# Top-32 attention and a gated feed-forward layer: shifts of exp on ScalarE, late reads, one reciprocal a duo

## The chip, the cores and the metric

The kernel runs on one core of a Trainium2 chip. The core has five engines with queues of their own, each of which works its instructions in order: TensorE (matmul, PE in the profile), VectorE (DVE), ScalarE (ACT), GpSimd (POOL) and SyncE (SP), which issues the transfers. The metric is the device time of one execution in microseconds, the median of several runs.

## What is computed

```python
# q, k, v: (8, 8, 576, 64)
scores = (1 / sqrt(64)) * q @ k.transpose(0, 1, 3, 2)
kth    = 32nd largest score of each row
scores = where(scores >= kth, scores, -1e9)
attn   = exp(scores - max(scores))
attn   = attn / (sum(attn) + 1e-9)
x      = (attn @ v), heads side by side      # (4608, 512)
h      = x @ w_in                            # (4608, 2048)
g      = h * clip(h + 3, 0, 6) / 6
out    = g @ w_out                           # (4608, 512)
```

The two weight matrices arrive as 64-bit floats; the kernel makes 32-bit floats of them itself, out of the two 32-bit words of each.

## The kernel before, in words

**Tiling.** There are 8 batches of 8 heads. Two heads make a pair, so a batch has 4 pairs. The 576 rows of a head are four tiles of 128 rows and a rest of 64. A *duo* is two pairs (four heads) at one tile of rows. `Duo` has an index `u` (0 or 1) for the pair and `t` (0 or 1) for the head in the pair. A duo of the rest has half as much to do. A batch has 8 full duos and 2 of the rest; there are 80 duos.

**One duo.** `scores` has TensorE write scores into the one large PSUM tile (`big`, one buffer), and ScalarE copies them to `sc` in SBUF (L233, L236). `top` finds the 32 largest of each row on VectorE with four rounds of MAX8 (L250) and three of MATCH_REPLACE8 (L254). `shift` forms (32nd largest - largest) x scale, on GpSimd (L263, L266). `exp` on ScalarE flattens what lies below the 32nd value (L273), takes the exponential with its sum into `den` (L278) and adds a small constant (L283). `inverse` is VectorE's reciprocal of `den` (L287). `weights` on GpSimd multiplies by it (L297) and splits the 32-bit words into 16-bit halves (L306). `flip` transposes these by a transfer (L312), and `join` puts the halves together again as `eT` (L318), on ScalarE for u = 0 and on GpSimd for u = 1. `values` multiplies them with v on TensorE (L338, `pv`), and `place` has ScalarE copy the result into `xT` (L348), or `xr` for rests.

**Feed-forward.** 128 finished rows make a block. `feed_forward` is a generator that is worked in 16 pieces: 8 pieces compute `h` (L365), 512 columns in every two pieces, then 8 sum `acc` over w_out (L385). After each 512 columns of h, ScalarE reads h twice (L373, L375); `gate` on GpSimd follows two pieces later (L379, L380). After the last piece, ScalarE scales `acc` into `o` (L395), and SyncE writes it out.

**Order of the work.** It is written out by hand, and no scheduler changes it. Each duo has 8 slots, one for each round of `top`; the loop at L564 goes through them. The tables `usual`, `behind`, `early`, `soon` (L532 to L545) say at which slot, counted from the duo's first, each step of the duo is issued; a number over 7 is a slot of a later duo. A slot issues the round of `top`, the steps that are due (`parts`, those named shift first), a step of the weights' conversion as long as there is one, at slot 1 the scores of the next duo, and then pieces of feed-forward: about one a slot, somewhat more if over 24 pieces are left (L597). So values of a duo stand at its slot 22 (`usual`), or at slot 25 and thus behind the scores issued at slot 25 (`behind`, from the second batch on until four duos from the end).

**Conversion.** `convert` loads 512 columns (L102), takes the magnitude and the low word on ScalarE into `a` and `y` (L108, L111), clamps on GpSimd (L109), and combines on VectorE (L117, L118) and GpSimd (L123). There are 16 pieces of w_in, then 16 of w_out, one step each slot during the first four duos.

Of the kernel before, what the change touches and what calls it, by code (L numbers as in the profile page):

```python
# [16 lines left out]
TOP_K = 32  # L17
# [12 lines left out]
def kernel(  # L30
# [65 lines left out]
    def convert(dst, src):  # L96
# [10 lines left out]
        y = gpool.tile([P, WC], F32, tag="g", name="y")  # L107
# [7 lines left out]

        au, yu = a[:].bitcast(U32), y[:].bitcast(U32)
        nc.vector.tensor_scalar(au, au, 3, None, ALU.logical_shift_left)  # L117
        nc.vector.scalar_tensor_tensor(  # L118
            out=yu, in0=hi, scalar=0x80000000, in1=yu,
# [4 lines left out]
            dst.bitcast(I32), a[:].bitcast(I32), y[:].bitcast(I32), ALU.add  # L124
# [14 lines left out]
    class Pair:  # L139
# [6 lines left out]
        def load(self):  # L146
            h0 = 2 * self.hp
            t = self.landed = kqpool.tile([P, 2 * J + 1, 2, D], F32, tag="kq", name="landed")
            for i, src in enumerate((k, q)):
                for hh in range(2):  # L150
                    nc.sync.dma_start(
                        t[:, i * J : (i + 1) * J, hh, :],
                        src[self.b, h0 + hh, 0:JP, :].rearrange("(p j) d -> p j d", j=J),
                    )
                nc.sync.dma_start(
# [29 lines left out]
    class Duo:  # L185
# [73 lines left out]
        def shift(self, u):  # L259

            nt, m = self.nt, self.m[u]
            d = self.less[u] = mpool.tile([P, 2], F32, tag="shift", name="shift")
            nc.gpsimd.tensor_tensor(  # L263
                d[:, 0:nt], m[:, 0:nt, TOP_K - 1], m[:, 0:nt, 0], ALU.subtract
            )
            nc.gpsimd.tensor_scalar_mul(d[:, 0:nt], d[:, 0:nt], scale)  # L266

        def exp(self, u):
# [7 lines left out]
            for t in range(nt):  # L276
                row = self.row(u, t)
                nc.scalar.activation(  # L278
                    row, row, AF.Exp, bias=self.less[u][:, t : t + 1], scale=-scale / FLAT,
                    accum_out=self.den[:, u, t : t + 1],  # L280
                )
            d = self.den[:, u, 0:nt]
            nc.scalar.activation(d, d, AF.Copy, bias=EPS)  # L283

        def inverse(self, u):
            d = self.den[:, u, 0 : self.nt]
            nc.vector.reciprocal(d, d)  # L287
# [64 lines left out]
    def feed_forward(xT, rows):  # L352
# [6 lines left out]
        for f0 in range(0, NFC, nf):  # L359
# [12 lines left out]
            g = gpool.tile([P, 512], F32, tag="g", name="g")  # L372
            nc.scalar.activation(g[:], h[:], AF.Relu, bias=three[:], scale=1.0)  # L373
            hs = hpool.tile([P, 512], F32, tag="h", name="hs")
            nc.scalar.copy(hs[:], h[:])  # L375
            gs.append(g)

            def gate(g=g, hs=hs):
                nc.gpsimd.tensor_scalar(g[:], g[:], 6.0, 0.0, ALU.min, ALU.max)  # L379
                nc.gpsimd.tensor_tensor(g[:], g[:], hs[:], ALU.mult)  # L380

            yield gate
        acc = ps_w.tile([P, DM], F32, tag="w", name="acc")
        for f in range(NFC):
# [7 lines left out]
            if f % 2 == 1:  # L392
                if f == NFC - 1:
                    o = opool.tile([P, DM], F32, tag="o", name="o")
                    nc.scalar.mul(o[:], acc[:], 1.0 / 6.0)  # L395
                    for p0, p1, dst in rows:
                        nc.sync.dma_start(dst, o[p0:p1, :])
                yield None

# [5 lines left out]
    for b in range(B):  # L405
        halves = [pairs[b][0:2], pairs[b][2:4]]
        for qt in range(J):
# [3 lines left out]
            if qt == (0 if b == B - 1 else J - 1) and not 2 < b < B - 1:  # L411
# [11 lines left out]
    gates = []  # L423

    def piece(count=1):
        nonlocal left
        for _ in range(count):
            while todo:
                try:
                    gates.append(next(todo[0]))  # L430
                    left -= 1
                    break
                except StopIteration:
                    todo.pop(0)
            else:
                gates.append(None)
            if len(gates) > 2:
                gate = gates.pop(0)
                if gate:
                    gate()  # L440
# [45 lines left out]
    def land(count=1):  # L486

        for _ in range(min(count, len(chunks))):
            c = convert(*chunks.pop(0))
# [20 lines left out]
    def pair_at(m, first):  # L510
# [5 lines left out]
    first[0].load()  # L516
# [16 lines left out]
        shift0=3, exp0=4, inverse0=9, weights0=10, flip0=12, join0=15,  # L533
        shift1=7, exp1=8, inverse1=13, weights1=14, flip1=16, join1=19, values=22, place=23,
# [101 lines left out]
```

## Time and profile before

| | |
|---|---|
| median of 3 runs | 1581.66 us (1581.61 to 1581.7) |
| span of the profiled execution | 1578.5 us |
| busy: TensorE, VectorE | 1456.9 us (92%), 1466.8 us (93%) |
| busy: GpSimd, ScalarE | 1144.5 us (73%), 1096.3 us (69%) |
| top-32: L250 and L254, all forms | 1519 us of instruction time, which overlaps |
| feed-forward on TensorE, L385 and L365 | 516.9 and 544.4 us |
| GpSimd's wait for `den` (L297) | 222.7 us |
| ScalarE's waits for h (L373) and for sums (L395) | 140.6 and 106.6 us |

How to read it: a busy share is a mean over the whole span; the slices, forty of 39.5 us each, show where it lies (a 9 is 90% or more). In lists of waits the engine and line that waited come first, then for what; the numbers are the total in us, the number of waits and the longest. In lists in order of time the columns are the start and the duration in us, the engine, the line, the operation and its operands, and in brackets the idle time before it and what ended that. TensorE's ends are modelled, so it may show as full with small gaps. A matmul of 32-bit floats shows as two records for each instruction, for instance 8 `acc` records for 4 instructions.

### The profile page before, as it was taken

The numbers are of one execution on the slowest core, as the hardware profiler recorded it, in microseconds if no ns is written. First come the engines' busy times: TensorE is split into PE (matmuls) and PEld (weight loads), VectorE is DVE, ScalarE is ACT, GpSimd is POOL, SyncE is SP. The second block draws the span as 40 slices with busy tenths as digits, with TensorE's granted clock in tenths as the row PEclk, the third lists the DMA queues.
The fourth block names the chain that finished last, engine by engine and source line by source line (L and its number), as shares of the span: only waits on it lengthen the run. The fifth ranks groups of instructions, "written<-read, shape, count | busy, mean of one in ns | idle before, by whom it ended". The sixth has DMA issues, their size and how long they took to land.

```text
span 1578.5 us, 28787 instructions
## 1 busy us (share of the span) xinstructions
PE 1456.9 (92%) x10272; PEld 1039.0 (66%) x10272; DVE 1466.8 (93%) x3105; ACT 1096.3 (69%) x1865; POOL 1144.5 (73%) x1264
## 2 busy tenths in 40 slices
PE   5256799979999999998999999999999999999899
PEld 3153566567767777666777777776777767677675
DVE  6999999999999999999999999999999999999700
ACT  6675777777777777777776786777766787777621
POOL 4868687777867777867687777867687777767841
PEclk9568999989999999999999999999999999999999
DMA  8652543444344543545254543446244443533410
GB/s 236 159 181 45 113 83 81 94 91 97 76 90 89 101 83 76 101 85 119 55 106 76 97 89 82 93 93 116 57 96 87 98 88 74 103 65 68 83 22 14
DMA packets 450319, 144.49 MB, mean 92 GB/s; under 512 B 433280, under 2 KB 441472, under 8 KB 450176
## 3 DMA queue, kind: packets, MB, share of 16 engines
q1 hardware_dynamic: 450176, 142.65, 43.5%
q8 instruction: 81, 1.33, 0.3%
q14 instruction: 62, 0.51, 0.1%
HBM read 45.09 MB, written 9.44 MB: 35 GB/s over the span
## 4 chain that ended last, share of the span: by engine, by line
DVE 51%; PE 35%; POOL 5%; issue 3%; ACT 3%; DMA 1%; SPq 1%; POOLq 0%; ACTq 0%; DVEq 0%
DVE m L250 26%; DVE wk L254 22%; PE h L365 14%; PE acc L385 13%; PE pv L338 4%; PE big L232 3%; POOL e L306 1%; DVE y L118 1%; POOL sc L297 1%; DMA t<-e 1%; POOL eT L318 1%; DVE a L117 1%; PE big L177 1%; ACT sc L278 1%; ACT eT L318 1%
## 5 line engine op out<-in xcount | busy, mean ns | idle before, releaser
L250 DVE MAX8 m<-wk 128x8 f32<-128x576 f32 x864 | 613.1, 746 | 2.2
L385 PE MATMUL acc<-w_out,g 128*128 128x512 f32 x1152 | 516.9, 600 | 14.1 <-POOL g L380 14.1
L365 PE MATMUL h<-xT,w_in 128*128 128x128 f32 x4096 | 485.5, 279 | 17.3 <-ACT xT L348 17.3
L365 PEld LDWEIGHTS h<-xT,w_in 128*128 128x128 f32 x4096 | 475.0, 195 | 39.5 <-issue 18.2
L254 DVE MATCH_REPLACE8 wk<-m,wk 128x576 f32<-128x576 f32 x576 | 423.7, 742 | 0.0
L385 PEld LDWEIGHTS acc<-w_out,g 128*128 128x128 f32 x1152 | 213.6, 191 | 260.4 <-issue 238.6
L297 POOL TENSOR_SCALAR sc<-sc,den 128x576 f32<-128x576 f32 x288 | 213.8, 753 | 229.9 <-DVE den L287 222.7
L306 POOL COPY e<-sc 128x2304 uint16<-128x2304 uint16 (+1 forms) x192 | 320.3, 1678 | 10.2
L278 ACT ACTIVATE sc<-sc,shift 128x576 f32<-128x576 f32 x288 | 220.4, 769 | 40.5 <-POOL shift L266 37.7
L318 ACT COPY eT<-t 128x2304 uint16<-128x2304 uint16 (+1 forms) x82 | 215.9, 2632 | 37.9 <-DMA t<-e 35.3
L273 ACT ACTIVATE sc<-sc,m 128x576 f32<-128x576 f32 x288 | 210.1, 777 | 46.2 <-DVE m L250 46.0
L338 PE MATMUL pv<-eT,vm 128*64 128x128 f32 (+1 forms) x2560 | 164.0, 273 | 57.9 <-ACT eT L318 45.8
L254 DVE MATCH_REPLACE8 wk<-m,sc 128x576 f32<-128x576 f32 x288 | 211.8, 742 | 0.0
L318 POOL COPY eT<-t 128x2304 uint16<-128x2304 uint16 (+1 forms) x78 | 203.8, 2613 | 6.9 <-DMA t<-e 6.5
L338 PEld LDWEIGHTS pv<-eT,vm 128*64 128x64 f32 x2560 | 135.2, 141 | 109.3 <-ACT eT L318 49.7
L250 DVE MAX8 m<-sc 128x8 f32<-128x576 f32 x288 | 203.3, 742 | 2.4 <-ACT sc L236 2.4
L373 ACT ACTIVATE g<-h,three 128x512 f32<-128x512 f32 x144 | 98.5, 684 | 150.0 <-PE h L365 140.6
L380 POOL TENSOR_TENSOR g<-g,hs 128x512 f32<-128x512 f32 x144 | 185.0, 1285 | 12.1 <-POOL g L379 0.2
L233 ACT COPY sc<-big 128x2048 f32<-128x2048 f32 (+1 forms) x65 | 119.3, 1836 | 26.1 <-PE big L232 26.0
L232 PE MATMUL big<-kq 64*128 64x512 f32 x512 | 136.4, 653 | 0.0
L379 POOL TENSOR_SCALAR g<-g 128x512 f32<-128x512 f32 x144 | 89.2, 620 | 62.6 <-ACT g L373 52.4
L395 ACT ACTIVATE o<-acc 128x512 f32<-128x512 f32 x36 | 21.4, 595 | 106.6 <-PE acc L385 106.6
(47 smaller groups left out, 1113.1 us busy)
## 6 DMA issues: line engine op xcount, KB each, us to landing
landed<-in_k_dram SPq DMA_DIRECT2D x64, 128.0 KB, 3.0
landed<-in_q_dram SPq DMA_DIRECT2D x64, 128.0 KB, 3.0
st<-in_moe_w_in_dram SPq DMA_DIRECT2D x16, 512.0 KB, 5.1
vm<-in_v_dram SPq DMA_DIRECT2D x64, 128.0 KB, 2.3
st<-in_moe_w_out_dram SPq DMA_DIRECT2D x16, 512.0 KB, 6.6
out_dram<-o SPq DMA_DIRECT2D x32, 256.0 KB, 2.4
t<-e SPq DMA_TRANSPOSE x160, 4.6
landed<-in_k_dram SPq DMA_DIRECT2D x32, 32.0 KB, 2.8
```

The lines of the kernel that those rows point to most:

```text
L232: nc.tensor.matmul(banks[:, 2 * i + hh, :], pr.qT[d, qs], pr.kT[d, :])
L250: nc.vector.max(self.m[u][:, t, 8 * r : 8 * r + 8], self.cur[t])
L254: nc.vector.match_replace(wk, self.m[u][:, t, 8 * r : 8 * r + 8], self.cur[t], LOWEST)
L273: nc.scalar.activation(row, row, AF.Prelu, bias=m[:, t, TOP_K - 1 : TOP_K], scale=-1.0, alpha=FLAT)
L278: nc.scalar.activation(row, row, AF.Exp, bias=self.less[u][:, t : t + 1], scale=-scale / FLAT, accum_out=self.den[:, u, t : t + 1],)
L297: nc.gpsimd.tensor_scalar(row, row, self.den[:, u, t : t + 1], 1.0, ALU.mult, ALU.mult)
L306: nc.gpsimd.tensor_copy(halves[:, :, to : to + c1 - c0], words)
L318: copy(eT[:, 0 : self.nb, :] .rearrange("p c q -> p (c q)") .bitcast(U16) .rearrange("p (x h) -> p h x", h=2), self.t16[u][:, 0 : 2 * self ...
L338: nc.tensor.matmul(pv[hh * D : (hh + 1) * D, u * w : (u + 1) * w], pr.vm[:, hh, c, :] if c < J else pr.vr[:, hh, :], rhs, start=(c == 0), ...
L365: nc.tensor.matmul(h[:, (f - f0) * P : (f - f0 + 1) * P], w_in[:, i, f * P : (f + 1) * P], xT[:, i, :], start=(i == 0), stop=(i == NHP - 1),)
L380: nc.gpsimd.tensor_tensor(g[:], g[:], hs[:], ALU.mult)
L385: nc.tensor.matmul(acc[:], gs[f // nf][:, f % nf * P : (f % nf + 1) * P], w_out[:, f, :], start=(f == 0), stop=(f == NFC - 1),)
```

## The change

Eight things change.

- **Shift**: its two steps move from GpSimd to ScalarE, as a scaled copy and one addition for each head.
- **Sums and reciprocals**: the small constant is added (`settle`) and the reciprocal taken once for both pairs of a duo, except in the first two and the last; both halves' weights follow that one reciprocal at slots 13 and 15.
- **Reads**: ScalarE's reads of h, and its copy of the finished sum, are queued one piece later, so that ScalarE doesn't stand waiting for TensorE.
- **Conversion**: for the first 16 pieces `y` is in PSUM, and VectorE writes its result to another tile.
- **First loads**: the q loads of the first pair are issued by ScalarE.
- **Values**: they are behind the scores (slot 25) from the fourth batch on instead of the second, and until eight duos from the end instead of four.
- **The end**: six duos have nearer slots (`soon`) instead of two, with a table for the last one.
- **Rests of the last batch**: they come after its second tile of rows instead of the first.

```diff
-        y = gpool.tile([P, WC], F32, tag="g", name="y")
+        y = (
+            ps_w.tile([P, WC], F32, tag="w", name="yp")
+            if early
+            else gpool.tile([P, WC], F32, tag="g", name="y")
+        )
...
+        ys = gpool.tile([P, WC], F32, tag="g", name="ys") if early else y
...
-            for i, src in enumerate((k, q)):
+            for i, (src, eng) in enumerate(((k, nc.sync), (q, queue or nc.sync))):
...
-            d = self.less[u] = mpool.tile([P, 2], F32, tag="shift", name="shift")
-            nc.gpsimd.tensor_tensor(
-                d[:, 0:nt], m[:, 0:nt, TOP_K - 1], m[:, 0:nt, 0], ALU.subtract
-            )
-            nc.gpsimd.tensor_scalar_mul(d[:, 0:nt], d[:, 0:nt], scale)
+            d = self.less[u] = mpool.tile([P, 2, 2], F32, tag="shift", name="shift")
+            nc.scalar.activation(d[:, 1, 0:nt], m[:, 0:nt, 0], AF.Copy, scale=-scale)
+            for t in range(nt):
+                nc.scalar.activation(
+                    d[:, 0, t : t + 1],
+                    m[:, t, TOP_K - 1 : TOP_K],
+                    AF.Identity,
+                    bias=d[:, 1, t : t + 1],
+                    scale=scale,
+                )
...
-            d = self.den[:, u, 0:nt]
+
+        def inverse(self, us):
+
+            d = self.den[:, us[0] : us[-1] + 1, 0 : self.nt]
+            nc.vector.reciprocal(d, d)
+
+        def settle(self, us):
+            d = self.den[:, us[0] : us[-1] + 1, 0 : self.nt]
             nc.scalar.activation(d, d, AF.Copy, bias=EPS)
...
-            yield gate
+            def read(h=h):
+                g = gpool.tile([P, 512], F32, tag="g", name="g")
+                nc.scalar.activation(g[:], h[:], AF.Relu, bias=three[:], scale=1.0)
+                hs = hpool.tile([P, 512], F32, tag="h", name="hs")
+                nc.scalar.copy(hs[:], h[:])
+                gs.append(g)
...
+            yield read
...
+        def write():
+            o = opool.tile([P, DM], F32, tag="o", name="o")
+            nc.scalar.mul(o[:], acc[:], 1.0 / 6.0)
+            for p0, p1, dst in rows:
+                nc.sync.dma_start(dst, o[p0:p1, :])
+
+        yield write
...
-            if qt == (0 if b == B - 1 else J - 1) and not 2 < b < B - 1:
+            if qt == (1 if b == B - 1 else J - 1) and not 2 < b < B - 1:
...
+        reads.append(read)
+        if len(reads) > 1:
+            read = reads.pop(0)
+            gates.append(read() if read else None)
+        if len(gates) > 2:
+            gate = gates.pop(0)
+            if gate:
+                gate()
...
-        shift0=3, exp0=4, inverse0=9, weights0=10, flip0=12, join0=15,
-        shift1=7, exp1=8, inverse1=13, weights1=14, flip1=16, join1=19, values=22, place=23,
+        shift0=3, exp0=4, shift1=7, exp1=8, settle01=8, inverse01=13, weights0=13, weights1=15,
+        flip0=15, flip1=17, join0=18, join1=20, values=22, place=23,
...
     soon = dict(
-        shift0=3, exp0=3, inverse0=5, weights0=5, flip0=7, join0=10,
-        shift1=7, exp1=7, inverse1=9, weights1=9, flip1=11, join1=14, values=16, place=17,
+        shift0=3, exp0=4, shift1=7, exp1=8, settle01=8, inverse01=10, weights0=10, weights1=11,
+        flip0=12, flip1=13, join0=15, join1=16, values=18, place=18,
+    )
+    last = dict(
+        shift0=3, exp0=3, settle0=3, inverse0=5, weights0=5, flip0=7, join0=10,
+        shift1=7, exp1=7, settle1=7, inverse1=8, weights1=8, flip1=9, join1=11, values=11, place=11,
     )
...
+            when = behind if 3 * per_batch <= m < ND - 8 else usual
...
+            if not left:
+                piece()
```

## The prediction

> **What bounds the kernel now.** I read the busy shares and the slices of the span first, then the waits of VectorE and TensorE, then TensorE in order of time around its waits, and last the end of the chain.
>
> ```profile
> PE 1456.9 (92%) x10272; PEld 1039.0 (66%) x10272; DVE 1466.8 (93%) x3105; ACT 1096.3 (69%) x1865; POOL 1144.5 (73%) x1264
> PE   5256799979999999998999999999999999999899
> DVE  6999999999999999999999999999999999999700
> ...
> PEclk9568999989999999999999999999999999999999
> ```
>
> Two engines are full at once. VectorE works without a gap from 13.6 us until its last top-32 search ends near 1490.7 us. TensorE is idle a good deal in the first ten slices, full after them, and works alone at the end. Its work in program order, at the rates of its undisturbed stretches (0.112 us for a 128x128 record, 0.43 us for an `acc` record, 0.058 us for a `pv` record), sums to 1435 us. Its lag behind that sum is 117 us at 240 us, 136 us at 341 us and about 132 us from there to 1450 us. TensorE's losses after 200 us are few:
>
> ```profile
> 308.93 1.22 PE L226 MATMUL big<-kr,kq 128*128 128x128 f32 x4 [3.75 <-ACT sc L236]
> ...
> 326.75 14.81 PE L365 MATMUL h<-xT,w_in 128*128 128x128 f32 x108 [9.30 <-ACT xT L348]
> ...
> 1089.60 5.02 PE L365 MATMUL h<-xT,w_in 128*128 128x128 f32 x28 [3.39 <-ACT xT L348]
> ```
>
> At the first it waited for the copy of scores out of its large PSUM tile; at the other two it had no other feed-forward work queued and stood in the first matmuls of a block, whose `xT` ScalarE had not yet copied. ScalarE reached that copy at VectorE's pace; this is ScalarE in order of time:
>
> ```profile
> 321.21 1.44 ACT L273 ACTIVATE sc<-sc,m 128x576 f32<-128x576 f32 x2 [1.99 <-DVE m L250]
> ...
> 324.31 1.85 ACT L233 COPY sc<-big 128x2048 f32<-128x2048 f32 x1
> 326.05 0.38 ACT L236 COPY sc<-big 128x256 f32<-128x256 f32 x1
> 326.32 0.39 ACT L348 COPY xT<-pv 128x256 f32<-128x256 f32 x1
> ```
>
> So these spots set TensorE by VectorE's clock, and time that VectorE gains before 1089 us moves all that follows. VectorE itself hardly waits (13.3 us in two, of which 10.0 us is the start):
>
> ```profile
> DVE a L117 <- POOL a L109: 13.3, 2, 10.0
> DVE den L287 <- ACT den L283: 9.3, 4, 6.7
> DVE m L250 <- ACT sc L236: 2.4, 2, 1.7
> ```
>
> The end, first on ScalarE, then on GpSimd, then on the chain:
>
> ```profile
> 1490.68 1.44 ACT L273 ACTIVATE sc<-sc,m 128x576 f32<-128x576 f32 x2 [3.96 <-DVE m L250]
> 1496.14 0.77 ACT L278 ACTIVATE sc<-sc,shift 128x576 f32<-128x576 f32 x1 [4.02 <-POOL shift L266]
> ```
> ```profile
> 1498.31 1.47 POOL L297 TENSOR_SCALAR sc<-sc,den 128x576 f32<-128x576 f32 x2 [0.15 <-DVE den L287]
> ...
> 1506.62 2.76 POOL L318 COPY eT<-t 128x2304 uint16<-128x2304 uint16 x1 [0.55 <-DMA t<-e]
> ```
> ```profile
> 1512.72 2.33 PE pv L338 x40
> 1515.05 3.63 PE acc L385 x8
> 1518.68 14.29 PE h L365 x128
> 1532.97 13.74 PE acc L385 x32
> ```
>
> The last top-32 ends at 1490.7, its transposed weights are joined at 1509.4, the last `pv` starts at 1512.7, and behind it stand 8 `acc` records and two whole blocks of 14.29 + 13.74 = 28.03 us. The span ends 3.75 us after TensorE.
>
> [...] the weight conversion's two-input step (L118) takes 679 ns at the median and up to 1749 ns. [...] The 128x2 copy at L283 measures 203 ns, so a small copy is near 0.2 us[...]. [...] no PSUM read by VectorE is in this trace. [...] Here issuing k takes from 0.72 to 2.78 us and q only then starts, until 4.77 us.
>
> **Part by part.**
>
> *First loads.* The q loads of the first pair are issued on ScalarE beside k, so they are out at about 2.8 instead of 4.77 us. The first search waits for this chain: 2.0 us earlier. ScalarE's table load (1.28 us) moves behind the issue and still ends ahead of the first copy at 8.0.
>
> *Converted words in PSUM.* For the first 16 of 32 pieces L118 reads one operand from PSUM. Those 16 take 15.98 us now; undisturbed 16 x 0.68 = 10.9. Saved 5.1[...]: **4 us** (from 0[...], to 5).
>
> *One reciprocal a duo.* The order of the changed program has 83 instead of 160. Each delays the next search by 0.07 us (1409.23 to 1409.31 in the chain): 77 x 0.07 = **5.4 us** off VectorE, 4 of it by 1089 us. On GpSimd both halves' weights now follow one reciprocal; the second half's come up to one weights pass, 1.47 + 2.10 = 3.6 us, later. Transposes and joins hide that in the slots left before `pv`, except at the 72nd and 73rd duo, where I allow 1 to 3 us.
>
> *Shifts on ScalarE.* GpSimd loses 35.3 + 34.1 = 69 us[...]. Exp no longer waits for GpSimd (37.7 us in 26 waits). The price is about 0.6 us more in front of each exp, and that ScalarE stands at the shift until the search is over, with copies of scores, joins and `xT` behind it; those stood behind the exp in the next slot before, at most 2.4 us later. In `usual` the place of slot 23 stands behind shift1 of that slot. TensorE's next block waits for it.
>
> *Reads and sums a piece late.* ScalarE waited 140.6 us for h and 106.6 us for sums. No work goes away. What it is worth is in ScalarE being punctual: of VectorE's waits for ScalarE and GpSimd after the start (3.31 + 0.83 + 1.43 + 0.69 = 6.3 us) I take off 2, range 0 to 6.3.
>
> *Values behind scores from the fourth batch on.* In the second and third batch values come three slots earlier, so the `xT` copy at 326.3 stands only behind VectorE's slot 23, some 13 us earlier, and the losses of 3.75 and 9.30 us go. In program order TensorE is up to 7.7 us ahead until the 33rd duo and level at the 39th. There it waits again for VectorE, so what this part brings is that TensorE arrives punctually, no more.
>
> *The sum.* VectorE ends 2.0 + 4 + 5.4 + 2 = 13.4 us sooner, at 1477.3. From there to the last joined weights, with durations of this tail: shift 0.6, 1.44, exps and sum 1.86, reciprocal 0.3, weights 3.63, transpose 4.7, join 2.76 = 15.3 us (18.7 now, for want of GpSimd's shift): 1492.6. TensorE: at 1089.6 it gains 2 + 4 + 4 + 1 - 0.6 = 10 us, its wait of 4.41 us at 1495.7 goes, and 5.2 us of feed-forward now stand behind the last `pv` instead of ahead of it: 1512.7 - 10 - 4.4 - 5.2 = 1493. The two agree. Behind it: 2.33 + 20 x 0.43 + 56.1 + 3.75 = 70.8 us. Span 1563.8; the times lie 3.2 us above the span (1581.66 against 1578.5): **1567 us**.
>
> **Rivals.**
>
> *TensorE keeps its lag* (18%). Between 67 and 200 us it waits for joined weights, and those now come later in GpSimd's order. If it gains only 3 us by 1089, the last `pv` is at 1500 and the time 1500 + 70.8 + 3.2 = 1574. For it: TensorE is full for 1100 us and makes nothing good. Against: the two waits before 341 us leave 13 us of room.
>
> *ScalarE's order becomes the bound, slower* (12%). From 1090 us to the end TensorE has no slack. If both shifts of each of the 20 duos hold its copies by 0.55 us and all reaches TensorE, that is 22 us: 1567 + 22 = 1589. For it: copies of scores free the only large PSUM tile. Against: scores stand seven slots ahead of their search.
>
> *No change* (6%): the gains at VectorE end in new waits, 1579 to 1584.
>
> *All waits go* (6%): VectorE ends at 1473, TensorE arrives with it, and the time is 1567 - 4.3 = 1563, or 1556 if the tail's feed-forward also starts without a gap of 7 us.
>
> **How the numbers follow.** Forecast 58%, around 1567. Faster by over 0.2% (below 1578.5): forecast, first and last rival, 0.82; same 0.06; slower 0.12. The range leaves out the slower rival and part of no change, and reaches from 1556 to 1579.
>
> **What would show it.** VectorE's first search near 11.6 us;[...] VectorE's end near 1477; no wait of 9 us for `xT` near 320; TensorE's wait for `xT` still there near 725 and 1080; the last `pv` near 1493. It is wrong if TensorE waits anew for `pv` or for the score copies after 400 us, or if VectorE waits for `den`.

## The result and the profile after

The changed kernel took 1593.84 us (median of 4, 1590.67 to 1595.61) against 1581.63 us for the kernel before, a ratio of 1.0076 (95% interval 1.0058 to 1.0093). It is 12 us slower; the forecast was 1567 us. In the profiled execution the span is 1591.8 us.

The changed kernel's busy times, and two rows of its slices:

```profile
PE 1464.6 (92%) x10272; PEld 1041.1 (65%) x10272; DVE 1458.1 (92%) x3028; ACT 1163.8 (73%) x2236; POOL 1070.6 (67%) x944
...
PE   5266899799999999997999999998999999999989
...
DVE  6999999999899999999999999999999999989700
```

The work went where it was meant to go: VectorE has 8.7 us less, GpSimd 74 us less, ScalarE 68 us more. But VectorE's row has 8s now, and its last top-32 search ends at 1502.0 us, against 1491.3 in the kernel before. Its waits tell why:

```profile
DVE den L298 <- ACT den L302: 23.2, 10, 6.1
DVE a L123 <- POOL a L114: 10.2, 1, 10.2
DVE m L257 <- ACT sc L243: 9.9, 6, 2.6
```

The wait of 10.2 us is the start and the one of 6.1 us lies behind the last search; both were there before. What is left are 13 waits, 25.0 us, between the first search and the last, against 6.3 us before. In order of time they all lie in rest duos, or at the duo behind one. Four of them:

```profile
416.71 0.17 DVE L298 RECIPROCAL den<-den 128x2 f32<-128x2 f32 x1 [2.96 <-ACT den L302]
420.47 1.42 DVE L257 MAX8 m<-sc 128x8 f32<-128x576 f32 x2 [1.28 <-ACT sc L243]
```
```profile
1186.61 0.18 DVE L298 RECIPROCAL den<-den 128x4 f32<-128x4 f32 x1 [3.46 <-ACT den L302]
1189.81 1.42 DVE L257 MAX8 m<-sc 128x8 f32<-128x576 f32 x2 [0.73 <-ACT sc L243]
```

A slot of a full duo lasts 2.43 us of VectorE's time, a slot of a rest duo 1.4 us. From duo 4 on (counted from 0) the 59 full duos take 1144.0 us together (1144.8 before), the 16 rest duos 203.0 us (182.7 before). So the loss is in the rest duos. The table shows when VectorE's search of a duo starts, in us against the kernel before; duos 8, 9, 18, 19, 28, 29, 32 and so on are rests.

| search of duo | 2 | 8 | 10 | 20 | 30 | 33 | 58 | 68 |
|---|---|---|---|---|---|---|---|---|
| changed kernel | -3.5 | -8.8 | -6.2 | -2.2 | +1.1 | +3.4 | +2.4 | +8.4 |

All that was to be gained early was gained by duo 8, and lost again in the next seven rest duos. TensorE follows. Its lag, the start of a duo's scores less the work ahead of them in program order, as in the prediction:

| scores of duo | 9 | 16 | 35 | 38 | 62 | 79 |
|---|---|---|---|---|---|---|
| before | 117.3 | 136.6 | 131.0 | 131.6 | 134.4 | 131.9 |
| changed kernel | 112.5 | 127.7 | 132.7 | 139.2 | 145.1 | 144.7 |

The wait of 9.30 us for `xT` near 320 us is gone, as forecast, but most of its time comes back a little earlier, as a wait of TensorE for transposed weights, and behind it one of 2.24 us for `xT`:

```profile
309.18 1.98 PE L353 MATMUL pv<-eT,vm 128*64 128x128 f32 x16 [6.96 <-ACT shift L270]
...
316.11 4.13 PE L380 MATMUL h<-xT,w_in 128*128 128x128 f32 x22 [2.24 <-ACT xT L363]
```

(The shift named in the first is only what ScalarE did last; its join of these weights, from 306.37 to 309.13, stands right ahead of it.) So the 13.05 us of the two waits before became 9.20, and of the 9 us of lag that are gone at duo 16, 4.8 had gone by duo 9. Until duo 35 the gain is lost again; 6.8 us of that are seven waits of 0.3 to 1.3 us, at blocks' `xT` and at the `pv` of rest duos, where the kernel before has 0.5 us. The two steps up behind that are waits of TensorE for ScalarE, here in order of time:

```profile
730.78 1.22 PE L233 MATMUL big<-kr,kq 128*128 128x128 f32 x4 [7.37 <-ACT kr L190]
```
```profile
1115.19 3.14 PE L380 MATMUL h<-xT,w_in 128*128 128x128 f32 x13 [3.83 <-ACT hs L392]
```

At the first, `kr` stood in ScalarE's queue behind a join, a shift and the exponentials of a search, and ScalarE had come late to these because it had stood 2.96 and 3.00 us for TensorE just before. TensorE makes nothing good after the second: its lag at the end is 12.8 us above before, the span 13.3 us.

What stands behind 1115 us is seen queue by queue, SyncE's issues first, then GpSimd, then ScalarE:

```profile
1088.93 0.35 SPq L418 DMA_DIRECT2D out_dram<-o  x1
1089.40 2.80 SPq L327 DMA_TRANSPOSE t<-e  x1
1092.25 1.27 SPq L158 DMA_DIRECT2D landed<-in_k_dram  x2
...
1095.56 0.63 SPq L162 DMA_DIRECT2D landed<-in_q_dram  x1
1096.30 18.10 SPq L327 DMA_TRANSPOSE t<-e  x3
```
```profile
1087.38 2.10 POOL L321 COPY e<-sc 128x2304 uint16<-128x2304 uint16 x1
1101.93 2.78 POOL L333 COPY eT<-t 128x2304 uint16<-128x2304 uint16 x1 [12.45 <-DMA t<-e]
```
```profile
1111.93 1.86 ACT L240 COPY sc<-big 128x2048 f32<-128x2048 f32 x1 [7.66 <-POOL e L321]
```

The second half's weights were split by 1089.5 us, but its transpose was issued at 1096.3, behind the first half's (2.8 us) and six loads of the next batch's k and q, some 4 us of issue. The first half's was late itself: split by 1085.9, issued at 1089.4, because SyncE stood ahead of it at the output of a finished block, whose sum ScalarE scaled only at 1088.31. So the late copy of a sum, too, holds up a transpose here. In the kernel before, the second half's transpose was in slot 16, ahead of the loads in the same slot; now it is in slot 17. GpSimd stands 12.45 us at its join, the next weights and splits come after that, the copy of scores waits for their tile, and ScalarE's read of h behind that copy reaches TensorE 3.83 us late. GpSimd's waits for transposes rose from 6.5 us in 3 to 207.2 us in 55. This one cost time; which of the others did isn't seen from their sum (in the first run below it is 35.5 us, and the time no shorter).

### The profile page after: what moved, and what is told of

Same layout as the page of the kernel before. It is cut to its first block, busy times and chain, and to the rows that moved or that the text cites. A ratio compares the mean times of both kernels' runs of the same rounds, so it can differ in the third digit from the quotient of the medians.

```text
span 1591.8 us, 28774 instructions
## 1 busy us (share of the span) xinstructions
PE 1464.6 (92%) x10272; PEld 1041.1 (65%) x10272; DVE 1458.1 (92%) x3028; ACT 1163.8 (73%) x2236; POOL 1070.6 (67%) x944
## 4 chain that ended last, share of the span: by engine, by line
PE 60%; DVE 20%; POOL 7%; DMA 4%; issue 3%; ACT 3%; SPq 3%; POOLq 0%; ACTq 0%; DVEq 0%
PE acc L404 23%; PE h L380 22%; DVE m L257 10%; DVE wk L261 8%; PE pv L353 7%; PE big L239 5%; DMA t<-e 4%; POOL e L321 3%; POOL sc L312 2%; PE big L222 1%; POOL eT L333 1%; PE big L184 1%; PE big L233 1%; SPq L158 1%; DVE y L124 1%
## 5 line engine op out<-in xcount | busy, mean ns | idle before, releaser
L380 PE MATMUL h<-xT,w_in 128*128 128x128 f32 x4096 | 489.5, 280 | 14.5 <-ACT xT L363 8.9
L333 POOL COPY eT<-t 128x2304 uint16<-128x2304 uint16 (+1 forms) x78 | 203.7, 2612 | 214.6 <-DMA t<-e 207.2
L397 POOL TENSOR_TENSOR g<-g,hs 128x512 f32<-128x512 f32 x144 | 183.8, 1276 | 12.1
L272 ACT ACTIVATE shift<-m,shift 128x1 f32<-128x1 f32 x288 | 73.0, 289 | 36.2 <-DVE m L257 31.5
```

Of the source, the lines that this page charges most:

```text
L333: copy(eT[:, 0 : self.nb, :] .rearrange("p c q -> p (c q)") .bitcast(U16) .rearrange("p (x h) -> p h x", h=2), self.t16[u][:, 0 : 2 * self ...
L380: nc.tensor.matmul(h[:, (f - f0) * P : (f - f0 + 1) * P], w_in[:, i, f * P : (f + 1) * P], xT[:, i, :], start=(i == 0), stop=(i == NHP - 1),)
```

## Experiments

### One part of the change taken back

Times of one kernel here spread over 1 to 5.5 us, and the kernel before, run beside each series, has medians from 1580.8 to 1581.3 us; so a difference of 1 or 2 us says little.

Three theories of what costs the time: the single reciprocal with its later weights (A), the shifts on ScalarE (B), the reads a piece late (C). Beside them, the loads of the last paragraph. Each run is the changed kernel with one thing put back or, for the loads, moved.

Two sums and two reciprocals a duo, at the slots of before:

```diff
-        shift0=3, exp0=4, shift1=7, exp1=8, settle01=8, inverse01=13, weights0=13, weights1=15,
-        flip0=15, flip1=17, join0=18, join1=20, values=22, place=23,
+        shift0=3, exp0=4, settle0=4, inverse0=9, weights0=10, flip0=12, join0=15,
+        shift1=7, exp1=8, settle1=8, inverse1=13, weights1=14, flip1=16, join1=19, values=22, place=23,
```

> The changed kernel with one part undone: in the usual and behind tables each half of a duo has its own sum and reciprocal again (slots 4/9 and 8/13) and the weights, transposes and joins stand at the slots of before. Theory A (late weights: both halves' weights after slot 13, the second transpose after the loads in SyncE's queue, so GpSimd stands at the join, the next weights come late, ScalarE's copy of scores waits for the tile and all behind it comes late): 1572 to 1582 us, GpSimd's wait at the join for the transpose falls from 207 us to under 60, ScalarE's wait for GpSimd's split (43 us) goes. Theory B (ScalarE is late because of its own 70 us of new work and the shift's place in its queue): stays at 1588 to 1596 us. Theory C (reads of h a piece late hold the PSUM tiles): stays at 1588 to 1596.

Measured: 1595.57 us, ratio to before 1.0083 (1.0067 to 1.0098). The waits for a score tile held by GpSimd's split are nearly gone (2.9 us, 43.1 in the changed kernel), yet VectorE waits 29.3 us in 12 for `den` (23.2 in 10), and ScalarE stands 81.3 us in 65 at the shifts (31.5 in 34 in the changed kernel). Theory A alone falls.

The loads of the next batch two slots later:

```diff
-            if i == 0:
+            if i == 2:
                 p = pair_at(m, 4)
```

> The changed kernel, with only the loads of k and q of the next batch issued at slot 2 of a duo instead of slot 0, so that the second transpose (slot 17, which is slot 1) stands ahead of them in SyncE's queue. Theory A: the loads' issue of about 4 us no longer delays the transpose; 1580 to 1590 us, the longest wait at the join falls from 12.4 us to under 9. Theories B and C: no change, 1590 to 1596.

Measured: 1584.78 us, ratio 1.0026 (1.0016 to 1.0036): 9 us of the 12. At the same place GpSimd's wait is 6.82 us and ScalarE's 2.93, and TensorE's wait of 3.83 us is gone (SyncE, GpSimd and ScalarE in this kernel):

```profile
1087.29 5.69 SPq L327 DMA_TRANSPOSE t<-e  x2
1093.07 1.24 SPq L158 DMA_DIRECT2D landed<-in_k_dram  x2
```
```profile
1095.07 2.82 POOL L333 COPY eT<-t 128x2304 uint16<-128x2304 uint16 x1 [6.82 <-DMA t<-e]
```
```profile
1105.11 1.87 ACT L240 COPY sc<-big 128x2048 f32<-128x2048 f32 x1 [2.93 <-POOL e L321]
```

VectorE still loses 11.7 us from duo 8 to duo 33 (-9.0 to +2.7), so the loads are what is lost late, not what VectorE loses early. (The longest wait at a join, elsewhere, is still 12.1 us, where under 9 was expected.)

The shifts on GpSimd again:

```diff
-            nc.scalar.activation(d[:, 1, 0:nt], m[:, 0:nt, 0], AF.Copy, scale=-scale)
...
+            nc.gpsimd.tensor_tensor(
+                d[:, 0, 0:nt], m[:, 0:nt, TOP_K - 1], m[:, 0:nt, 0], ALU.subtract
+            )
+            nc.gpsimd.tensor_scalar_mul(d[:, 0, 0:nt], d[:, 0, 0:nt], scale)
```

> The changed kernel with the shift back on GpSimd, all else as changed. Theory B: ScalarE is 90 us lighter and punctual, 1575 to 1584 us, VectorE's wait for den falls from 23 us to about 9. Theory A: GpSimd, which stands at the join, makes the shift late as well: 1592 to 1605. Theory C: 1590 to 1596.

Measured: 1592.48 us, ratio 1.0068 (1.0052 to 1.0083). Theory B alone falls too: ScalarE then waits 58.8 us for GpSimd's shifts, as theory A had it.

The reads at once again:

```diff
-        if len(reads) > 1:
+        if len(reads) > 0:
...
-            if not left:
-                piece()
```

> The changed kernel with the reads of h and of the finished sum queued at once again, and without the extra piece where none is left. Theory C: the waits for the second read of h (5.6 us in two) and what follows go, 1582 to 1587 us. Theory A: these waits are a consequence of the late copy of scores; at most 4 us better, and ScalarE waits for TensorE again: 1589 to 1600. Theory B: 1592 to 1600.

Measured: 1605.88 us, ratio 1.0148 (1.0131 to 1.0165), slower than all three theories allow. Within the change the late reads are worth 12 us; theory C is refuted.

### One part of the change alone

If no part taken back restores the time, each may cost by itself. These are the kernel before with one hunk of the change, nothing else.

> The kernel before with one part of the change alone: ScalarE's reads of h and of sums queued a piece late, and a piece counted where none is left. Taken out of the whole change, this part cost 12 us (1605.9 against 1593.8). Theory Q (the loss comes from the order of SyncE's and GpSimd's queues in the short slots of the rest duos, that is from the single reciprocal with its later weights, and the reads are a gain): 1570 to 1577, ScalarE's waits for h nearly gone. Rival S (ScalarE is what comes too late in the rest duos, and the late reads only help there because the shifts are on it): 1580 to 1583, no change.

```diff
-            yield gate
+            yield read
...
+        reads.append(read)
+        if len(reads) > 1:
+            read = reads.pop(0)
+            gates.append(read() if read else None)
```

Measured: 1585.7 us, ratio 1.003 (1.0019 to 1.004). Here they cost 4.4 us, against both expectations. TensorE stands 4.00 us for a read of h at 664.05 and is 6.5 us later from duo 35 on. What that does to VectorE is seen at the rest duo near 1180 us, first ScalarE, then VectorE:

```profile
1175.78 0.60 ACT L401 ACTIVATE o<-acc 128x512 f32<-128x512 f32 x1 [1.85 <-PE acc L389]
1179.35 0.69 ACT L375 ACTIVATE g<-h,three 128x512 f32<-128x512 f32 x1 [2.98 <-PE h L365]
```
```profile
1186.30 0.17 DVE L287 RECIPROCAL den<-den 128x2 f32<-128x2 f32 x1 [2.76 <-ACT den L283]
```

A late TensorE makes ScalarE stand at a sum and at h, with the exponentials queued behind; in a rest duo, with its short slots, VectorE is at the reciprocal before they are done, and pays. So the two engines hold each other up, through ScalarE's order.

> The kernel before with the shifts of exp on ScalarE alone. Theory Q: the shift is 0.5 to 0.8 us of ScalarE's work for two waits for GpSimd removed, so within 3 us of the time before (1579 to 1585). Rival S (ScalarE too late in the rest duos): 1586 to 1592, with VectorE's waits at the reciprocals grown from 9 us to over 18 us.

```diff
-            nc.gpsimd.tensor_scalar_mul(d[:, 0:nt], d[:, 0:nt], scale)
...
+            nc.scalar.activation(d[:, 1, 0:nt], m[:, 0:nt, 0], AF.Copy, scale=-scale)
+            for t in range(nt):
+                nc.scalar.activation(
+                    d[:, 0, t : t + 1],
...
+                    bias=d[:, 1, t : t + 1],
```

Measured: 1593.78 us, ratio 1.0084 (1.0067 to 1.0101), the way rival S said and past its range. VectorE waits 18.6 us for `den`, and ScalarE stands 98.2 us in 81 at the shift.

> The kernel before with the conversion's y in PSUM for the first 16 chunks and the first q loads on ScalarE's queue. VectorE is then some 8 us ahead after the eighth duo. If nothing later takes it back: 1573 to 1576. If the slack of the loads and the rest duos is what takes it back whatever else is changed (theory Q says that it does only behind the later weights, rival S only behind the shifts): 1580 to 1583.

```diff
+            ps_w.tile([P, WC], F32, tag="w", name="yp")
+            if early
+            else gpool.tile([P, WC], F32, tag="g", name="y")
...
+    first[0].load(nc.scalar)
```

Measured: 1576.18 us, ratio 0.997 (0.9959 to 0.9981). VectorE is 4.2 us early at duo 2 (not the 8 us that were expected) and 4.3 us early at duo 68: with the order of before, nothing later takes an early gain away.

> The kernel before with one settle and one reciprocal per duo and the later weights, transposes and joins that come with it (the change's usual table, values behind scores as before). Theory Q: the second transpose then stands behind six loads in SyncE's queue and in the rest duos the weights come too late: 1587 to 1595, and VectorE's waits for the reciprocal's input over 15 us. Rival S: 1577 to 1582, the 83 reciprocals instead of 160 worth some 4 us less what a few waits give back.

```diff
+        shift0=3, exp0=4, shift1=7, exp1=8, settle01=8, inverse01=13, weights0=13, weights1=15,
+        flip0=15, flip1=17, join0=18, join1=20, values=22, place=23,
```

Measured: 1590.77 us, ratio 1.0063 (1.0048 to 1.0078), as theory Q said. Shifts, reciprocal and late reads cost 12.5, 9.5 and 4.4 us one by one, the first hunk brings 5.1, and the sum, 21 us, is not the 12 of the whole change. Both Q and S hold for one part each; neither is the whole. The later values and the last duos were not run alone on the kernel before.

### Places in the queues

If the parts are good and their places bad, moving them by a slot or two must show it.

> The kernel before with the shifts on ScalarE, but queued in the slot of the exponential (4 and 8) and no longer a slot ahead of it (3 and 7), so that ScalarE does the piece's reads of that slot before it stands at the shift for VectorE's fourth search. With the shift a slot ahead this kernel took 1593.8 against 1581.3. If that loss comes from where the shift stands in ScalarE's queue: 1580 to 1586, ScalarE's waits for VectorE under 60 us instead of 98. If it comes from the work itself (288 and 160 small instructions, 0.5 to 0.8 us a unit) in the rest duos: 1590 to 1596.

```diff
-        shift0=3, exp0=4, inverse0=9, weights0=10, flip0=12, join0=15,
-        shift1=7, exp1=8, inverse1=13, weights1=14, flip1=16, join1=19, values=22, place=23,
+        shift0=4, exp0=4, inverse0=9, weights0=10, flip0=12, join0=15,
+        shift1=8, exp1=8, inverse1=13, weights1=14, flip1=16, join1=19, values=22, place=23,
```

Measured: 1588.43 us, ratio 1.0045 (1.003 to 1.006), between the two expectations: 5.4 of the 12.5 us are the place (ScalarE's waits at the shift fall from 98.2 to 61.8 us).

> The kernel before with one settle and one reciprocal a duo and the later weights (1590.8 with that alone), and the next batch's k and q loads in slot 2 instead of 0, so that the second transpose no longer stands behind six loads in SyncE's queue. If the loads between the transposes are what the late weights cost: 1580 to 1584. If it is the later weights and values themselves, in the short slots of the rest duos: 1588 to 1592.

```diff
+        shift0=3, exp0=4, shift1=7, exp1=8, settle01=8, inverse01=13, weights0=13, weights1=15,
+        flip0=15, flip1=17, join0=18, join1=20, values=22, place=23,
...
-            if i == 0:
+            if i == 2:
                 p = pair_at(m, 4)
```

Measured: 1581.13 us, ratio 1.0001 (0.9992 to 1.0009). With the loads behind both transposes the single reciprocal costs nothing; it brings nothing either, since VectorE's 3.3 us of lead at duo 8 are lost by duo 30. What the loads in slot 2 do to the kernel before by themselves was not run.

> The whole change with two moves: loads in slot 2 (1584.8 with that alone, against 1593.8) and the shifts in the slot of the exponential. If the shift's place in ScalarE's queue cost the change what it cost alone: 1572 to 1579, below the time before. If the late reads have already taken away what the early shift holds up: 1583 to 1587.

```diff
-        shift0=3, exp0=4, shift1=7, exp1=8, settle01=8, inverse01=13, weights0=13, weights1=15,
+        shift0=4, exp0=4, shift1=8, exp1=8, settle01=8, inverse01=13, weights0=13, weights1=15,
...
-            if i == 0:
+            if i == 2:
                 p = pair_at(m, 4)
```

The table `soon` has the same two shifts moved. Measured: 1576.96 us, ratio 0.9975 (0.9965 to 0.9984): 7.8 us less than with the loads alone. VectorE's 16 rest duos take 185.3 us instead of 194.1. ScalarE's waits at the shift fall only from 38.1 to 26.0 us, so it is hardly the sum of these waits that the place changes.

> The whole change with loads in slot 2 and with the values behind scores from the second batch on, as in the kernel before, instead of from the fourth. This leaves the change without its values part in batches two and three. If the values in slot 22 there were worth something (TensorE's first waits for transposed sums are shorter): 1587 to 1595. If they cost what VectorE loses at the rest duos of those batches: 1576 to 1582. Within 1583 to 1587: the part is worth nothing either way.

```diff
-            when = behind if 3 * per_batch <= m < ND - 8 else usual
+            when = behind if per_batch <= m < ND - 8 else usual
...
-            if i == 0:
+            if i == 2:
                 p = pair_at(m, 4)
```

Measured: 1576.57 us, ratio 0.9971 (0.9961 to 0.9981): 8.2 us less than with the loads alone. The values part of the change is a loss. With values in slot 22 in the second and third batch, this is ScalarE ahead of a double rest at 400 us, and VectorE in it (the kernel with the loads moved only):

```profile
398.28 0.60 ACT L416 ACTIVATE o<-acc 128x512 f32<-128x512 f32 x1 [4.53 <-PE acc L404]
```
```profile
402.94 0.18 DVE L298 RECIPROCAL den<-den 128x4 f32<-128x4 f32 x1 [1.06 <-ACT den L302]
417.05 0.17 DVE L298 RECIPROCAL den<-den 128x2 f32<-128x2 f32 x1 [2.85 <-ACT den L302]
```

With values behind scores neither reciprocal there waits, and VectorE is 5.1 us earlier at duo 20 (-6.8 against -1.7). TensorE's wait for `xT` near 320 us is back (9.32 us), and the time is shorter all the same.

### All three moves, and parts taken out again

> The whole change with three moves: loads in slot 2, shifts in the slot of the exponential, values behind scores from the second batch on. The first with one of the other two took 1577.0 and 1576.6. If TensorE's idle time decides, and the two take away the same idle time in the first batches (TensorE is set back to VectorE's place near 320 us and again near 730 us in both): 1574 to 1577. If what they take away adds up: 1568 to 1573.

```diff
-        shift0=3, exp0=4, shift1=7, exp1=8, settle01=8, inverse01=13, weights0=13, weights1=15,
+        shift0=4, exp0=4, shift1=8, exp1=8, settle01=8, inverse01=13, weights0=13, weights1=15,
...
-            when = behind if 3 * per_batch <= m < ND - 8 else usual
+            when = behind if per_batch <= m < ND - 8 else usual
...
-            if i == 0:
+            if i == 2:
                 p = pair_at(m, 4)
```

Measured: 1574.37 us, ratio 0.9956 (0.9941 to 0.9971). The two moves are worth 7.8 and 8.2 us singly and 10.4 together: mostly the same idle time.

> As the kernel with the three moves, but with the last duos as in the kernel before (rest duos of the last batch behind its first query tile, the table of the last two duos, values behind scores up to the fourth duo from the end). In the changed kernel's traces TensorE idles some 2.5 us more than before at duos 75 to 79. If that is the table of the last six duos: 2 to 4 us less than the three moves alone. If the shorter chain behind the last duo pays for it: equal within 1 us or slower.

```diff
-            if qt == (1 if b == B - 1 else J - 1) and not 2 < b < B - 1:
+            if qt == (0 if b == B - 1 else J - 1) and not 2 < b < B - 1:
...
+        when = early if m < 2 else soon if m >= ND - 2 else behind if per_batch <= m < ND - 4 else usual
```

This is shown against the changed kernel, beside the three moves; `soon` has its slots of before. Measured: 1566.58 us, ratio 0.9908 (0.9891 to 0.9924): 7.8 us less, more than either expectation, and the best of all kernels here, ahead of both given ones. VectorE ends at the same time as with the three moves alone (1482 us); the gain lies behind that. TensorE in the changed kernel, behind VectorE's end at 1502.0:

```profile
1511.60 1.98 PE L404 MATMUL acc<-w_out,g 128*128 128x512 f32 x4
1514.82 1.09 PE L353 MATMUL pv<-eT,vm 128*64 128x128 f32 x16 [1.24 <-ACT eT L333]
...
1519.82 1.98 PE L353 MATMUL pv<-eT,vm 128*64 128x128 f32 x16 [3.69 <-POOL eT L333]
...
1522.15 9.75 PE L404 MATMUL acc<-w_out,g 128*128 128x512 f32 x20
```

and with the three moves and the end of before, behind 1481.9:

```profile
1484.32 1.09 PE L353 MATMUL pv<-eT,vm 128*64 128x128 f32 x16 [1.27 <-POOL eT L333]
...
1485.56 3.84 PE L380 MATMUL h<-xT,w_in 128*128 128x128 f32 x32
1489.24 10.46 PE L404 MATMUL acc<-w_out,g 128*128 128x512 f32 x24
1499.63 1.09 PE L353 MATMUL pv<-eT,vm 128*64 128x128 f32 x16
```

In the second, 32 records of h and 24 of `acc` fill the wait for the last weights, and from VectorE's end to the end of the span it takes 83.6 us. In the changed kernel 4 records of `acc` are left to fill it and 20 stand behind the last `pv`: TensorE idles 4.9 us, runs the next 12 us at a mean granted clock of 0.83, and it takes 89.8 us. The three moves alone show the same: 4.9 us idle, 20 records behind the last `pv`, 90.5 us. Which of the three things put back at the end does it was not told apart.

> As the kernel with the three moves, but with the shifts on GpSimd as before. If a shift on ScalarE, once it stands in the right place, is worth the two waits for GpSimd that it saves: 1 to 4 us slower than the three moves. If the 1.2 us a duo that it adds to ScalarE is a loss in the rest duos even there: 1 to 4 us faster.

```diff
-            nc.scalar.activation(d[:, 1, 0:nt], m[:, 0:nt, 0], AF.Copy, scale=-scale)
...
+            nc.gpsimd.tensor_tensor(
+                d[:, 0, 0:nt], m[:, 0:nt, TOP_K - 1], m[:, 0:nt, 0], ALU.subtract
+            )
+            nc.gpsimd.tensor_scalar_mul(d[:, 0, 0:nt], d[:, 0, 0:nt], scale)
```

Measured: 1589.94 us, ratio 1.0057 (1.0042 to 1.0072), far outside both expectations: 15.6 us slower. ScalarE waits 261.9 us in 68 for GpSimd's shifts. In the slot of the exponential they stand behind the second half's weights in GpSimd's queue, first GpSimd, then ScalarE:

```profile
1352.74 1.47 POOL L307 TENSOR_SCALAR sc<-sc,den 128x576 f32<-128x576 f32 x2
1354.27 2.10 POOL L316 COPY e<-sc 128x2304 uint16<-128x2304 uint16 x1
1356.34 0.20 POOL L270 TENSOR_TENSOR shift<-m 128x2 f32<-128x2 f32 x1
```
```profile
1356.88 0.78 ACT L285 ACTIVATE sc<-sc,shift 128x576 f32<-128x576 f32 x1 [5.93 <-POOL shift L273]
```

So this is the price of that place on GpSimd, not of GpSimd: with shifts on GpSimd a slot earlier the kernel with one reciprocal and later loads took 1581.13. The three moves with shifts on GpSimd a slot earlier were not run.

> As the kernel with the three moves, but with ScalarE's reads of h and of sums at once, as before. Within the changed kernel the late reads were worth 12 us, on the kernel before they cost 4.4 us. If they are worth what they were in the changed kernel because the shifts and the loads stood in the wrong place there: now within 3 us of the three moves. If they are worth it because a read at once stands at the head of ScalarE's queue for TensorE while the shift waits behind it: 8 to 14 us slower.

```diff
-        if len(reads) > 1:
+        if len(reads) > 0:
...
-            if not left:
-                piece()
```

Measured: 1578.32 us, ratio 0.9982 (0.9974 to 0.999): the late reads are worth 4.0 us there, between the two expectations.

> The changed kernel with only the last duos as in the kernel before: rest duos of the last batch behind its first query tile, one table for the last two duos, values behind scores up to the fourth duo from the end. In the kernel with the three moves this took off 7.8 us, all behind VectorE's last search, where TensorE then has 32 records of h and 24 of acc to do while the last weights come. If that holds whatever went before: 1584 to 1588. If the changed kernel's TensorE, 20 us later than with the moves, has work left there anyway: 1590 to 1594.

```diff
-            if qt == (1 if b == B - 1 else J - 1) and not 2 < b < B - 1:
+            if qt == (0 if b == B - 1 else J - 1) and not 2 < b < B - 1:
...
-            when = behind if 3 * per_batch <= m < ND - 8 else usual
+        when = early if m < 2 else soon if m >= ND - 2 else behind if per_batch <= m < ND - 4 else usual
```

`soon` has its slots of before. The last line also puts values behind scores from the second batch on, which the expectation doesn't speak of. Measured: 1578.97 us, ratio 0.9985 (0.9978 to 0.9992), 14.9 us less than the changed kernel and below both expectations. VectorE ends 8.0 us sooner (1494.0), as where, with the loads moved, the values part alone was taken back, and the way from there to the end is 83.6 us instead of 89.8. So both losses are there with the loads and shifts in their first places too, and they add up.

> As the kernel with the three moves and the last duos of before (1566.6), but with two sums and two reciprocals a duo, at the slots of the kernel before, except in the last two duos, which have two anyway. If the 75 reciprocals less are worth their 0.07 us each on VectorE up to the spots where TensorE waits for it: 1570 to 1573. If the later weights of one reciprocal take that away again: 1564 to 1567.

Shown against the kernel with the three moves and the last duos of before:

```diff
-        shift0=4, exp0=4, shift1=8, exp1=8, settle01=8, inverse01=13, weights0=13, weights1=15,
-        flip0=15, flip1=17, join0=18, join1=20, values=22, place=23,
+        shift0=4, exp0=4, settle0=4, inverse0=9, weights0=10, flip0=12, join0=15,
+        shift1=8, exp1=8, settle1=8, inverse1=13, weights1=14, flip1=16, join1=19, values=22, place=23,
```

Measured: 1586.48 us, ratio 1.0047 (1.0032 to 1.0062), 19.9 us slower, outside both expectations. VectorE is 5.4 us behind the best kernel at duo 4 already, standing 4.56 us for a clamped chunk from GpSimd at 137.69, and TensorE stands 5.21 us for a read of h at 664.37, where the late reads on the kernel before stood 4.00. The rest is lost mostly in rest duos (194.4 us against 182.1): from duo 37 on VectorE waits 14.5 us for `den` in six of them. At three of these (735.52, 828.15, 1188.06) ScalarE's join, which is in slot 15 there and not in 18, takes 2.8 us right ahead of the shift and the exponentials; that this is the cause was not tested.

The runs side by side, in us: the time, VectorE's 16 rest duos, and the way from VectorE's last search to the end of the span. The full duos take 1143.4 to 1144.8 us in all of them.

| kernel | time | rest duos | to the end |
|---|---|---|---|
| before | 1581.6 | 182.7 | 87.2 |
| changed | 1593.8 | 203.0 | 89.8 |
| loads later | 1584.8 | 194.1 | 89.1 |
| loads and shifts | 1577.0 | 185.3 | 89.6 |
| loads and values | 1576.6 | 185.7 | 89.2 |
| three moves | 1574.4 | 184.2 | 90.5 |
| three moves, last duos of before | 1566.6 | 182.1 | 83.6 |
| the same, two reciprocals | 1586.5 | 194.4 | 83.6 |

## Why the prediction was wrong

**The step that failed** is VectorE's waits: "of VectorE's waits for ScalarE and GpSimd after the start (3.31 + 0.83 + 1.43 + 0.69 = 6.3 us) I take off 2, range 0 to 6.3". They grew to 25.0 us. That is 20.7 of the 26.8 us by which the forecast was off. Behind it is a sentence that was not costed, that transposes and joins hide the later weights "in the slots left before `pv`". The prediction gives these slots no length; in the rest duos they last 1.4 us, not 2.43, and there a wait ahead of an exponential in ScalarE's queue reaches VectorE's reciprocal. It isn't that ScalarE is full: around the first three double rests it is busy 70 to 78% of the time (213 to 240, 393 to 422 and 575 to 604 us). It stands for others at the head of its queue, as at 398.28 us in the run with the loads moved. The prediction's own sign of being wrong came true: VectorE waits for `den`, and TensorE anew for `pv` after 400 us (0.84 to 1.32 us each, at 423 and 604 us).

Term by term. VectorE's end: forecast 1477.3, measured 1502.0. Of these 24.7 us, 20.7 are the waits, 2.2 the first loads, 0.7 the busy time, and 0.6 a reading: the prediction counts from 1490.7, where ScalarE takes over, and VectorE's last search ends at 1491.3. Some 0.5 are not accounted for. From there to the last half of the last `pv`: forecast 15.7 (there for the whole of it), measured 17.8; ScalarE's join of the half before, 2.78 us at 1502.22, stands ahead of the last exponentials and was not in the sum. Behind that: forecast 70.8, measured 72.0. Time above the span: forecast 3.2, measured 2.0. Together 24.7 + 2.1 + 1.2 - 1.2 = 26.8.

*First loads: nothing instead of 2.0 us.* The first search starts at 13.78 us (13.59 before). The issue of q ends at 2.75 us instead of 4.77. But issued from two engines at once, k and q land together, at 6.04 and 5.85 us: TensorE's first transpose waits for k until 6.01 us, where it had k at 4.54 and q at 6.67 before. The issue time saved was counted in full, and the trace shows none of it at the first search.

*Converted words in PSUM: right.* The early 16 took 10.8 us at 673 ns each instead of 15.96, saving 5.2 where 4 was forecast, since the prediction took some 1 us off its 5.1 for reads from PSUM, the author's estimate, which no trace showed; 0.65 us came back at VectorE's step ahead of it (L123 takes 11.86 us in the early half, 11.21 before). Alone, with the loads, this hunk is worth 5.1 us of time.

*One reciprocal: right in size on VectorE, wrong in what hides its price.* The busy time fell by 8.7 us together with the conversion, against 9.4. Its later weights and transposes put the second transpose behind six loads; this part cost 9.5 us on the kernel before and nothing once the loads had moved. In the best kernel it is worth 19.9 us.

*Shifts on ScalarE: the cost was named, and then not summed.* The additions took 289 ns, the copies 204 to 209, where the prediction put a small copy near 0.2 us; ScalarE is busy 1163.8 us (1096.3 before). "ScalarE stands at the shift until the search is over" is what happens: alone the part costs 12.5 us, of which 5.4 go with one slot later, and within the change that slot is worth 7.8.

*Reads a piece late: right in direction.* They are worth 12 us in the change and 4.0 with the moves, though they cost 4.4 us on the kernel before.

*Values: wrong in sign.* The waits of 3.75 and 9.30 us near 310 and 320 us went, but 9.20 us of waits came in their place, so some 4 us were won there and not 13. ScalarE then stood for sums ahead of the double rests, VectorE lost what it had gained, and TensorE waited again at 730.78. The part that was to bring "that TensorE arrives punctually, no more" cost 8.2 us, measured with the loads moved.

*The end: not priced.* The prediction moved 5.2 us of feed-forward from ahead of the last `pv` to behind it, as if that were neutral, and had TensorE's wait of 4.41 us there go. It did not go: TensorE idles 1.24 and 3.69 us there. What stood ahead fills the wait for the last weights.

The rivals. *ScalarE's order becomes the bound*, with 12% and 1589 us, is the nearest, and its engine is the right one; its place only in part, since 12.2 us of VectorE's lead are lost in rest duos before 660 us, where the rival looked behind 1090. That TensorE waits for ScalarE again near 725 and 1090 us was right (7.37 us at 730.78, 1.34 at 1094.95), though the first wait was for `kr` and not for `xT`; it is a way by which early losses reach TensorE. *No change* has the mechanism in its few words, "the gains at VectorE end in new waits"; it only has too few of them. *TensorE keeps its lag* did not happen by duo 16.

The sum of parts was attainable: with loads, shifts, values and last duos at other places the same parts take 1566.58 us. Of VectorE's waits between the first search and the last 6.7 us are then left, about as much as before. That the number is the forecast's is in part chance, since the way from VectorE's end to the end of the span is 2.9 us shorter than the 86.5 forecast and VectorE's end 4.6 us later than 1477.3.

## What to carry to other kernels

Where the order of work is written in slots, put each slot's length in us beside the table, and look at the shortest slots first: here all the new waits between the first search and the last lay in rest duos or right behind them. For each edit that queues something earlier or later, list what is queued behind it on that engine, transfers too, and follow that to the two engines that are full; a part that is a loss in the old order may be a gain in another (one reciprocal: 9.5 us lost on the kernel before, 19.9 gained in the best kernel). Leave work for the last wait: feed-forward moved behind the end of the chain no longer fills it.

## What the runs showed of the hardware

In the changed kernel TensorE's idle of 4.9 us behind VectorE's end cost more than itself. Behind the wait of 3.69 us at 1519.82 half a `pv` took 1.98 us instead of 1.09, and the granted clock from 1517.2 to 1524.0 was 0.50 (0.83 from 1520.0 to 1531.7); in the best kernel it stayed at 1.00 there. The clock fell 1.0 us into this wait, behind one of 1.24 us, and in the kernel before it was 0.50 from 724.6 to 727.9 us, behind a wait of 2.33.

The conversion's VectorE instruction with two tensor operands (128x512) was no slower with one of them in PSUM: 673 ns each in the early 16, against 679 ns at the median before. None of the 16 took over 680 ns; of the same 16 before, six took 1092 to 1747.
